# Splitting a decode over two steps: pieces of the first attention batch issued by engine, with two more raw weight tiles

## The chip, the cores and the metric

The kernel runs on one core of a Trainium2 chip. The metric is the device time of one execution in microseconds (us), as the median of several runs; shorter is better. Five engines work side by side, each through its own queue in order: PE (matrix multiplies, with PEld for its weight loads), DVE (vector work), ACT (activations), POOL and SP (here SP issues nearly all DMAs). An instruction that waits for another engine holds back everything behind it in its own queue.

## The reference, cut to what matters

Attention with rotary embedding, then a dense two-layer block, then a mixture of eight experts with one expert per row:

```python
# q, k, v: (4 batches, 8 heads, 576 rows, 64)
scores = matmul(rotate(q), rotate(k).T) / 8
attn   = softmax(scores) @ v                    # -> x (2304, 512)
h = x @ w_in; g = maximum(0.01 * h, h)          # w_in (512, 2048)
x = g @ w_out                                   # w_out (2048, 512)
e = argmax(cosine(x, expert_emb) / tau); p = softmax(...)[e]
out = p * (relu(x @ w1[e]) @ w2[e])
```

All inputs are float32, except that `w_in` and `w_out` come as pairs of 32-bit words, each tile of 128 x 512 numbers as 128 x 1024 words (512 KB): the kernel has to put the float32 number together from both words.

## The kernel before, in words

**Stages.** Attention goes through 16 pairs of heads (four pairs a batch), nine units a pair, one unit a step: 144 steps. The first four pairs (`WHOLE = 4`, the first batch, steps 0 to 35) are done in float32, the others in split float16. The dense block starts as soon as its weights and the rows of the first batch are there (from step 37 on) and then runs inside the attention steps; the experts come last.

**Side work of the first batch.** In steps 0 to 35 three kinds of side work are mixed in: the 32 raw weight tiles are decoded (`weights`, `decode`), the queries and keys of the next pair are rotated and turned (`prep_whole`), and the finished rows are scaled (`x_done`). Each is a generator that yields a `Piece` ahead of some instructions: with its cost on ACT (`A=`) and DVE (`V=`), `x=True` if it needs PE and the one PSUM buffer `t`, or `must=True` if it has to free that buffer next. A weight tile goes through: DMA; ACT L192 and L194; DVE L196 and L198; for `w_in` also ACT L220 (square sum), PE L185 (total), DVE L90 to L92 (a power of two as scale); then ACT L228 or L211 (high part) and DVE L230 or L213 (low part). Four jobs (`NW = 4`) decode at the same time, each with a raw tile of its own.

**Order.** Every step emits instructions in the order of the letters of a string. For the first batch that is `ORDER_W = 'HXtEFVCWsTsxs'`: H ACT copies the turned unit (L605), X DVE scales the scores and takes the row extreme (L575), t DVE copies the rest of the turned unit (L609), E ACT exponential (L580), F DVE finishes a unit (L645 to L649), V PE multiplies with the values (L627), C PE scores of the next two units (L551), W PE matmuls that only keep its clock up (L613), T PE turns the unit (L599). `s` is a call of `slot()`, which lets every job run one piece, and `x` one that runs PE pieces; a step also begins with `slot(must=True)`. So a job can run its ACT piece at one `s` and the DVE piece that needs it at the next `s` of the same step. `budget` caps what the decoding may issue in a step.

Of the kernel before, what the change touches and what calls it, by code (L numbers as in the profile page):

```python
# [41 lines left out]
TLOAD = 4  # L42
BUR = 1.5
WARM = 9
ORDER_W = 'HXtEFVCWsTsxs'
ORDER1 = 'HXEsFVWsLsxCs'
ORDER_A = 'ESXFHshLlVxsC'
ORDER_B = 'GXEKFHs2LVxsCo'
# [19 lines left out]
class Job:  # L68


    def __init__(self, gen):
        self.gen, self.live = gen, True
        self.run()

    def run(self):
# [21 lines left out]
def attention_moe_kernel(ctx: ExitStack, tc: tile.TileContext, qkv, w_in, w_out, emb, tau, w1, w2,  # L97
# [103 lines left out]
    slices = deque((f, o) for f in range(NF) for o in (0, 1))  # L201

    def weights(i):
        while slices:
            f, o = slices.popleft()
            raw = wp.tile([128, 512, 2], U32, name=f"raw{i}")
            if o:
                nc.sync.dma_start(out=raw.rearrange("p f t -> p (f t)"), in_=w_out32[128 * f:128 * f + 128, :])
                r = yield from decode(raw)
                yield Piece(A=0.75, when=lambda: f in M.scaled)  # L210
                nc.scalar.activation(out=wo[:, 0, f], in_=r, func=AF.Copy, scale=uw[:, f:f + 1])  # L211
                yield Piece(V=0.6)
                nc.vector.scalar_tensor_tensor(out=wo[:, 1, f], in0=r, scalar=uw[:, f:f + 1], in1=wo[:, 0, f].bitcast(F32), op0=ALU.mult, op1=ALU.subtract)  # L213
            else:
                nc.sync.dma_start(out=raw.rearrange("p (c f) t -> p c (f t)", c=4),
                                  in_=w_in32[:, 256 * f:256 * f + 256].rearrange("(c p) f -> p c f", p=128))
                w = yield from decode(raw)
                sq = small.tile([128, 1], F32, name="wsq", bufs=NW)
                yield Piece(A=0.86)
                nc.scalar.activation(out=junk[:, 0:512], in_=w, func=AF.Square, accum_out=sq, saturate=False)  # L220
                pb = yield from total(sq, 1)
                yield Piece(must=True, V=0.2)
                s = _pow2(nc, small, pb[:, 0:1], 1, uw[:, f:f + 1])
                M.scaled.add(f)
                hi = wi[:, 0, :, 128 * f:128 * f + 128]
                wv = w.rearrange("p (c f) -> p c f", c=4)
                yield Piece(A=0.75)
                nc.scalar.activation(out=hi, in_=wv, func=AF.Copy, scale=s)  # L228
                yield Piece(V=0.6)
                nc.vector.scalar_tensor_tensor(out=wi[:, 1, :, 128 * f:128 * f + 128], in0=wv, scalar=s, in1=hi, op0=ALU.mult, op1=ALU.subtract)  # L230
            M.wdone[o].add(f)
            yield Piece()
# [53 lines left out]
    def m_outs():  # L286
        while M.out:
            m_out(*M.out.pop(0))
# [379 lines left out]
    def x_done(b, c, x):  # L668

        ch = chunk[b, c]  # L670
        j = block_of[b, c]
        yield Piece(A=0.61, when=lambda: j < cur_block() + (2 * XTB if decoded() else XTB))
        sq = small.tile([128, 1], F32, name="xsq")
        nc.scalar.activation(out=junk[:, 0:512], in_=x, func=AF.Square, scale=2.0 ** 0.5, accum_out=sq, saturate=False)
        yield Piece(V=0.5)
        s = _pow2(nc, small, sq, 1, ux[:, ch:ch + 1])
        yield Piece(A=0.61)
        x16 = mp.tile([128, 2 * DM], F16, name="x16", bufs=X16)
        nc.scalar.activation(out=x16[:, 0:DM], in_=x, func=AF.Copy, scale=s)
        yield Piece(V=0.66)  # L680
        nc.vector.scalar_tensor_tensor(out=x16[:, DM:], in0=x, scalar=s, in1=x16[:, 0:DM], op0=ALU.mult, op1=ALU.subtract)
        t = blocks[j].index((b, c))
        if j not in xT:
            xT[j] = new_xt(j)
        nc.sync.dma_start_transpose(out=xT[j][:, :, 128 * t:128 * t + 128], in_=x16)
        xwait.discard(c)
        yield Piece()
        M.done.add((b, c))
        while M.ready < len(blocks) and all(z in M.done for z in blocks[M.ready]):
            M.ready += 1  # L690
# [353 lines left out]
                q.popleft()  # L1044
        return [z for z in [*list(xjobs)[:2], L.prep, *list(vjobs)[:1], *list(rjobs)[:1], *wjobs] if z is not None and z.live]

    def slot(x=False, must=False):
        used = dict(A=0.0, V=0.0)
        for z in jobs():
            p = z.nxt  # L1050
            if p.x != x or M.step < p.at or M.tick < p.tick or (p.when is not None and not p.when()):
                continue
            if x and L.x == M.tick:
                continue
            if p.must != must:
                continue
            if not p.must and z in wjobs and any(budget[e] <= 0 for e in p.cost):
                continue
            if not p.must and any(used[e] >= SLIM for e in p.cost):
                continue  # L1060
            for e, c in p.cost.items():
                budget[e] -= c
                used[e] += c
            if x:
                L.x = M.tick
            z.begun = True
            z.run()

    def step(i):

        M.tick += 1
        M.step = i if i is not None else M.step
        rate = RATE1 if M.unit == 0 else RATE2 if any(z.live for z in wjobs) else RATE3
        for e in budget:
            budget[e] = min(budget[e] + rate[e], BUR * rate[e])
        now = i is not None and 0 <= i < n
        prv = i is not None and 0 <= i - 1 < n
        due = [j for j in (i - LAGW, i - LAG) if 0 <= j < n and (j == i - LAGW) == (units[j][0] < WHOLE)] if i is not None else []
        slot(must=True)
        whole = now and units[i][0] < WHOLE  # L1080
        turned = prv and units[i - 1][0] < WHOLE
        second = M.second
        for z in ORDER_W if whole else ORDER1 if rate is RATE1 and (turned or not m_ready()) else ORDER_B if second else ORDER_A:
            if z == "E" and whole:
                a_exp(*e_[i])
            elif z == "E" and prv and not turned:
                a_exp(*e_[i - 1])
            elif z == "W":
                L.w = ps_h()
                if whole:  # L1090
                    keep_warm(0 if units[i][1] in (1, 3, 5, 8) else WARM // 2 if units[i][1] == 7 else WARM)
                elif i is not None:
                    keep_warm(WARM)
            elif z == "T" and whole:
                a_turn(i)
            elif z == "t" and turned:
                a_turned_end(*end_)
            elif z == "S":
                m = m_s1()
                M.second = bool(m or M.g or M.s)  # L1100
                if m:
                    M.h = m
            elif z == "X" and now:
                e_[i] = a_max(*units[i], ps_[i])
            elif z == "F" and L.fin and i is not None:
                a_fin(*L.fin)
                L.fin = None
            elif z == "H" and turned:
                end_ = a_turned(i - 1)
                if not whole:  # L1110
                    a_turned_end(*end_)
            elif z == "H" and prv:
                p = a_hi(e_[i - 1][0])
            elif z == "L" and prv and not turned:
                a_lo(e_.pop(i - 1)[0], p)
                pt_[i - 1] = a_transpose(p)
            elif z == "V" and due:
                g, u = units[due[0]]
                if u % 2 == 0:
                    L.o = ps_o()  # L1120
                a_pv(g, u, pt_.pop(due[0]), L.o)
                if u % 2 or u == 8:
                    L.fin = (g, u, L.o)
            elif z == "G" and M.h:
                m_g(M.h)
            elif z == "K" and M.h:
                m_leaky(M.h)
                M.g, M.h = M.h, None
            elif z == "h" and M.g:
                m_gh(M.g)  # L1130
            elif z == "l" and M.g:
                m_gl(M.g)
                M.s, M.g = M.g, None
            elif z == "C" and i is not None and 0 <= i + 1 < n:
                a_scores(i + 1)
            elif z == "2":
                M.second = False
                if M.s:
                    m_s2(M.s)
                    M.s = None  # L1140
            elif z == "o":
                m_outs()
            elif z == "x":
                slot(x=True)
            elif z == "s":
                slot()
        if R.late:
            slot()
            slot()

    wjobs += [Job(weights(i)) for i in range(NW)]
    rjobs.append(Job(directions()))
    M.step = -1
    for _ in range(PRE):
# [231 lines left out]
```

## Time and profile before

| | |
|---|---|
| median of 3 runs | 1030.99 us (1028.44 to 1032.89) |
| the profiled execution | 1032.32 us, span 1030.5 us |
| from the first X (L575) of step 0 to that of step 36 | 28.87 us to 191.88 us |
| busy in 22 to 192 us: PE / PEld / DVE / ACT | 131.99 / 107.22 / 129.55 / 122.20 of 170 us |
| granted PE clock in that stretch | 0.92 |

Read it like this: the profile page's busy shares are means over the whole span. The change touches the first batch alone, so the numbers that matter are those of its stretch. The idle time of an engine there is put down, wait by wait, to the engine that ended it.

### The profile page before, as it was taken

The numbers are of one execution on the slowest core, as the hardware profiler recorded it, in microseconds if no ns is written. First come the engines' busy times: TensorE is split into PE (matmuls) and PEld (weight loads), VectorE is DVE, ScalarE is ACT, GpSimd is POOL, SyncE is SP. The second block draws the span as 40 slices with busy tenths as digits, with TensorE's granted clock in tenths as the row PEclk, the third lists the DMA queues.
The fourth block names the chain that finished last, engine by engine and source line by source line (L and its number), as shares of the span: only waits on it lengthen the run. The fifth ranks groups of instructions, "written<-read, shape, count | busy, mean of one in ns | idle before, by whom it ended". The sixth has DMA issues, their size and how long they took to land. (4 is left out here: it accounts for less than half of the span.)

```text
span 1030.5 us, 20176 instructions
## 1 busy us (share of the span) xinstructions
PE 936.0 (91%) x7428; PEld 769.6 (75%) x7428; DVE 776.4 (75%) x1632; ACT 672.3 (65%) x1081; POOL 64.3 (6%) x64
## 2 busy tenths in 40 slices
PE   3678877899998779999899999999999999999996
PEld 2566756577886667887878888888877788888884
DVE  5786877977887867987888856422667998999992
ACT  5666777855666755766776555423256898888882
POOL 0000000000000000000000000000001462111110
PEclk9998988999998889999999999999999999999998
DMA  6333336557587667878688755200323111116190
GB/s 204 118 122 121 99 118 174 105 101 155 94 166 161 132 152 137 138 150 174 120 172 162 124 105 95 56 1 22 125 94 121 47 46 52 42 43 204 61 331 19
DMA packets 223624, 120.09 MB, mean 117 GB/s; under 512 B 194711, under 2 KB 204439, under 8 KB 223520
## 3 DMA queue, kind: packets, MB, share of 16 engines
q1 hardware_dynamic: 220320, 108.79, 45.0%
q0 software_dynamic: 3200, 9.97, 2.8%
q8 instruction: 60, 0.98, 0.4%
q14 instruction: 44, 0.36, 0.1%
HBM read 120.04 MB, written 10.49 MB: 127 GB/s over the span
## 5 line engine op out<-in xcount | busy, mean ns | idle before, releaser
L252 PEld LDWEIGHTS <-wi 128*128 128x128 f16 x1920 | 171.8, 99 | 26.9 <-issue 6.1
L282 PE MATMUL acc<-wo,gh 128*128 128x512 f32 x576 | 154.4, 411 | 2.7 <-ACT gh L266 2.6
L580 ACT ACTIVATE E<-E,amx 128x576 f32<-128x576 f32 x144 | 110.7, 769 | 34.1 <-DVE E L575 33.8
L259 ACT ACTIVATE g<-h 128x512 f32<-128x512 f32 x72 | 43.0, 598 | 136.1 <-PE h L252 57.1
L282 PEld LDWEIGHTS acc<-wo,gh 128*128 128x128 f32 x576 | 105.3, 192 | 27.1 <-ACT gh L266 4.9
L575 DVE TENSOR_SCALAR_CACHE_REDUCE E<-S,sc 128x576 f32<-128x576 f32 x108 | 87.8, 813 | 42.2 <-PE S L568 28.6
L252 PE MATMUL h<-xT,wi 128*128 128x256 f16 (+1 forms) x1152 | 113.6, 257 | 0.0
L588 DVE SCALAR_TENSOR_TENSOR P<-E,P 128x576 f16<-128x576 f32 x108 | 81.2, 752 | 16.0 <-ACT P L584 15.6
L584 ACT ACTIVATE P<-E 128x576 f16<-128x576 f32 x108 | 73.9, 684 | 29.3 <-DMA PT<-P 26.1
L252 PE MATMUL h<-xt,wi 128*128 128x256 f16 x768 | 90.7, 275 | 2.0 <-DMA xt<-x 2.0
L627 PEld LDWEIGHTS <-PT 128*128 128x128 f16 (+1 forms) x1680 | 61.4, 100 | 25.5 <-issue 14.9
L282 PE MATMUL acc<-wo,gl 128*128 128x512 f32 x288 | 77.4, 391 | 0.0
L627 PE MATMUL o<-v,PT 128*128 128x65 f16 (+3 forms) x1680 | 70.1, 194 | 7.5 <-DMA PT<-P 7.5
L566 PE MATMUL S<-stk 128*128 128x288 f16 (+1 forms) x240 | 61.2, 294 | 12.1 <-DVE E L575 10.1
L262 DVE SCALAR_TENSOR_TENSOR g<-h,g 128x512 f32<-128x512 f32 x72 | 49.5, 688 | 29.2 <-ACT g L259 29.1
L270 DVE TENSOR_TENSOR gl<-g,gh 128x512 fp32r<-128x512 f32 x72 | 49.4, 686 | 25.9 <-ACT gh L266 16.0
L282 PEld LDWEIGHTS acc<-wo,gl 128*128 128x128 f32 x288 | 54.5, 189 | 12.2
L995 PE MATMUL h<-w,hth 128*128 128x512 f32 x176 | 55.3, 395 | 0.4 <-ACT hth L979 0.4
L266 ACT ACTIVATE gh<-g 128x512 fp32r<-128x512 f32 x72 | 44.5, 618 | 15.1 <-PE acc L282 14.2
L551 PE MATMUL S<-qk 64*128 64x288 f32 (+1 forms) x96 | 30.1, 510 | 22.7 <-DVE ET L609 20.4
L568 PE MATMUL S<-stk,zq 128*128 128x288 f16 (+1 forms) x200 | 49.2, 292 | 0.0
L627 PE MATMUL o<-v,ET 128*128 128x65 f32 (+1 forms) x400 | 49.0, 275 | 0.0
(257 smaller groups left out, 1965.4 us busy)
## 6 DMA issues: line engine op xcount, KB each, us to landing
rb<-in_w SPq DMA_DIRECT2D x78, 512.0 KB
ra<-in_w SPq DMA_DIRECT2D x76, 512.0 KB
raw<-in_qkv SPq DMA_DIRECT2D x15, 640.0 KB
raw<-in_w_in SPq DMA_DIRECT2D x16, 512.0 KB
raw<-in_w_out SPq DMA_DIRECT2D x16, 512.0 KB
x2s<-x SPq DMA_DIRECT2D x18, 256.0 KB
raw<-in_qkv SPq DMA_DIRECT2D x14, 320.0 KB
v<-v SPq DMA_DIRECT2D x12, 162.5 KB
```

What stands on the lines that cost most here:

```text
L252: nc.tensor.matmul(m.h[:, c0:c1], lhsT=wi[:, a, c, 128 * f:128 * f + 128], rhs=xT[j][:, 4 * b_ + c, 0:c1 - c0], start=(n == 0), stop=(n == ...
L262: nc.vector.scalar_tensor_tensor(out=m.g, in0=m.h, scalar=0.01, in1=m.g, op0=ALU.mult, op1=ALU.max)
L270: nc.vector.tensor_tensor(out=m.gl, in0=m.g, in1=m.gh.bitcast(F32), op=ALU.subtract)
L282: nc.tensor.matmul(M.acc[:, t], lhsT=g_[:, tt], rhs=wo[:, a, f], start=(f == 0 and n == 0), stop=(f == NF - 1 and n == 2))
L566: nc.tensor.matmul(ps[o:o + m, n, 0:288], lhsT=stk[:, h, c0:c0 + m], rhs=stk[:, 2 + h, ks], start=True, stop=False)
L568: nc.tensor.matmul(ps[o:o + m, n, 0:288], lhsT=pairs[g][3][:, h, c0:c0 + m], rhs=stk[:, 4, ks], start=False, stop=True)
L575: nc.vector.tensor_scalar(out=e[:, 0:S].rearrange("p (a b) -> p a b", a=2), in0=ps[:, :, 0:288], scalar1=-0.125 if g < WHOLE else pairs[g] ...
L580: nc.scalar.activation(out=e[:, 0:S], in_=e[:, 0:S], func=AF.Exp, scale=-1.0, bias=mx)
L584: nc.scalar.activation(out=p[:, 0:576], in_=e[:, 0:S], func=AF.Copy, scale=TWO15)
L588: nc.vector.scalar_tensor_tensor(out=p[:, 576:1152], in0=e[:, 0:S], scalar=TWO15, in1=p[:, 0:576], op0=ALU.mult, op1=ALU.subtract)
L627: nc.tensor.matmul(o[ob:ob + m, 256 * h:256 * h + w], lhsT=pt[:, i, q0:q0 + m], rhs=v[:, j, h, c:c + w], start=(n == 0), stop=(n == len(to ...
L995: nc.tensor.matmul(OP[kk], lhsT=h_[:, c, :], rhs=wt[a][c // 2][:, 512 * (c % 2):512 * (c % 2) + 512], start=(n == 0), stop=(n == len(todo) ...
```

## The change

Four edits. The step order of the first batch names its calls by engine: `m` is a must call, `v` runs pieces that have DVE work or no cost, `a` pieces that have ACT work only. A job whose last piece in this step was one kind may not run one of the other kind in the same step (`z.last`); the jobs for finished rows are exempt. There are two `x` calls a step in place of one, open as long as no must piece is pending. Two further decode jobs take the two `xT` buffers as raw tiles until eight tiles are left to start, and the finished rows wait for these jobs. The higher budget (`RATE1`) ends with step 35.

```diff
-ORDER_W = 'HXtEFVCWsTsxs'
+ORDER_W = 'HXtEFxVCWmvvaTax'
+SPARE = 8
...
     def weights(i):
-        while slices:
+        while len(slices) > (SPARE if i >= NW else 0):
             f, o = slices.popleft()
-            raw = wp.tile([128, 512, 2], U32, name=f"raw{i}")
+            if i < NW:
+                raw = wp.tile([128, 512, 2], U32, name=f"raw{i}")
+            else:
+                raw = mp.tile([128, 8, 256], F16, name="xT", bufs=XTB) ...
...
-        yield Piece(A=0.61, when=lambda: j < cur_block() + (2 * XTB if decoded() else XTB))
+        yield Piece(A=0.61, when=lambda: not any(z.live for z in wjobs[NW:]) and j < cur_block() + (2 * XTB if decoded() else XTB))
...
-    def slot(x=False, must=False):
+    def slot(x=False, must=False, kind=None):
...
-            if x and L.x == M.tick:
+            if x and any(y.nxt.must for y in jobs()):
                 continue
             if p.must != must:
                 continue
+            if kind and not must:
+                if p.cost and (kind not in p.cost or (kind == "A" and "V" in p.cost)):
+                    continue
+                if z.last[0] == M.tick and z.last[1] not in (None, kind) and z not in xjobs:
+                    continue
...
-        rate = RATE1 if M.unit == 0 else RATE2 if any(z.live for z in wjobs) else RATE3
+        rate = RATE1 if M.unit == 0 and (i is None or i < 9 * WHOLE) else RATE2 if any(z.live for z in wjobs) else RATE3
...
-    wjobs += [Job(weights(i)) for i in range(NW)]
+    wjobs += [Job(weights(i)) for i in range(NW + XTB)]
```

The lines of the changed file are numbered one to four higher (L192 is L193 there, L196 L197, L211 L215, L230 L234, L575 L579, L580 L584). Both programs issue the same instructions, 144 steps each; they differ in order from the beginning up to step 41, where the last tile is done in the changed one (step 40 in the old one), and are alike from step 42 on.

**The decode of two tiles on ACT and DVE, before.** ACT in step 15: the copy H, the exponential E, the two ACT operations of tiles 817 and 819.

```order
L605 ACTIVATE ET_857<-h_843 128x512
L580 ACTIVATE E1_118<-E1_118,amx_859 128x576
L192 ACTIVATE raw0_817<-raw0_817 128x512
L194 ACTIVATE raw0_817<-raw0_817,half_88 128x512
L192 ACTIVATE raw1_819<-raw1_819 128x512
L194 ACTIVATE raw1_819<-raw1_819,half_88 128x512
```

DVE in the same step 15, from X to the X of step 16:

```order
L575 TENSOR_SCALAR E1_118,amx_859<-S_837 128x576
L609 COPY ET_857<-S_837 128x128
L645 TENSOR_SCALAR rd_863<-o_787 128x2
L648 RECIPROCAL rd_863<-rd_863 128x2
L649 TENSOR_TENSOR x1_494<-o_787,rd_863 128x128
L196 SCALAR_TENSOR_TENSOR raw0_817<-raw0_817 128x512
L198 SCALAR_TENSOR_TENSOR raw0_817<-raw0_817 128x512
L196 SCALAR_TENSOR_TENSOR raw1_819<-raw1_819 128x512
L575 TENSOR_SCALAR E0_117,amx_898<-acc_838 128x576
```

L196 of tile 817 stands in the step in which ACT's L192 and L194 of that tile stand, ahead of the X of step 16.

**The same on ACT and DVE, after.** ACT in steps 16 and 17: tiles 862 and 864 in the one, 905 and 902 in the other.

```order
L609 ACTIVATE ET_915<-h_891 128x512
L584 ACTIVATE E0_117<-E0_117,amx_917 128x576
L193 ACTIVATE raw0_862<-raw0_862 128x512
L195 ACTIVATE raw0_862<-raw0_862,half_88 128x512
L193 ACTIVATE raw2_864<-raw2_864 128x512
L195 ACTIVATE raw2_864<-raw2_864,half_88 128x512
L609 ACTIVATE ET_952<-h_931 128x512
L584 ACTIVATE E1_118<-E1_118,amx_954 128x576
L193 ACTIVATE raw1_905<-raw1_905 128x512
L195 ACTIVATE raw1_905<-raw1_905,half_88 128x512
L193 ACTIVATE raw3_902<-raw3_902 128x512
L195 ACTIVATE raw3_902<-raw3_902,half_88 128x512
```

DVE in step 18, from X to the X of step 19:

```order
L579 TENSOR_SCALAR E0_117,amx_995<-S_968 128x576
L613 COPY ET_993<-S_968 128x128
L197 SCALAR_TENSOR_TENSOR raw0_862<-raw0_862 128x512
L197 SCALAR_TENSOR_TENSOR raw1_905<-raw1_905 128x512
L199 SCALAR_TENSOR_TENSOR raw0_862<-raw0_862 128x512
L199 SCALAR_TENSOR_TENSOR raw1_905<-raw1_905 128x512
L579 TENSOR_SCALAR E1_118,amx_1042<-acc_969 128x576
```

The DVE pieces of tiles 862 and 905 moved into a step behind that of their ACT pieces: two steps later for tile 862, one for 905.

**The scale on ACT and DVE, after.** ACT in step 21, whose last instruction is the square sum of tile 907:

```order
L609 ACTIVATE ET_1132<-h_1102 128x512
L584 ACTIVATE E1_118<-E1_118,amx_1134 128x576
L215 ACTIVATE wo_101<-raw1_905,uw_82 128x512
L232 ACTIVATE wi_100<-raw3_902,ps_1128 128x4x128
L224 ACTIVATE junk_86,wsq_1115<-xT_907 128x512
```

DVE from the X of step 21 to that of step 22; the scale `pt_1166` is that of tile 907 (from PE's `t_1164`):

```order
L579 TENSOR_SCALAR E1_118,amx_1134<-acc_1062 128x576
L613 COPY ET_1132<-S_1061 128x128
L234 SCALAR_TENSOR_TENSOR wi_100<-raw0_862,ps_1082,wi_100 128x4x128
L217 SCALAR_TENSOR_TENSOR wo_101<-raw2_864,uw_82,wo_101 128x512
L91 TENSOR_SCALAR pt_1166<-t_1164 128x1
L92 TENSOR_SCALAR ps_1167<-pt_1166 128x1
L93 TENSOR_SCALAR uw_82<-pt_1166 128x1
L579 TENSOR_SCALAR E0_117,amx_1173<-S_1143 128x576
```

This part has not moved: the scale still stands ahead of the next X, and needs the last ACT work of the step before. It stands so in twelve of the 36 steps after and in thirteen before.

## Rows read from the trace of the kernel before

**Rows 1.** The page, part 2: PE's busy tenths in 40 slices, and its granted clock.
```profile
PE   3678877899998779999899999999999999999996
...
PEclk9998988999998889999999999999999999999998
```

**Rows 2.** Windows: start:end, length, busy us (count) by engine, clock, DMA share, GB/s.
```profile
22.00:192.00 170.00, 131.99 (x949) 107.22 (x950) 129.55 (x349) 122.20 (x214) 0.35 (x3) 0.92 0.39 122
...
192.00:200.00 8.00, 6.90 (x61) 5.00 (x60) 7.50 (x24) 5.83 (x12) 0.12 (x1) 1.00 0.76 133
...
208.00:216.00 8.00, 8.00 (x73) 5.97 (x72) 5.48 (x12) 5.08 (x8) 0.00 (x0) 1.00 0.88 147
```

**Rows 3.** Waits of DVE in 22 to 192: us in total, times, longest.
```profile
DVE raw L196 <- ACT raw L194: 17.4, 14, 3.1
DVE wi L230 <- ACT wi L228: 9.9, 9, 1.4
DVE pt L90 <- PE t L185: 6.2, 6, 2.2
```

**Rows 4.** Timeline of DVE: start, us, instruction [idle before]; steps 0, 15, 16, 36.
```profile
28.87 0.75 DVE L575 TENSOR_SCALAR_CACHE_REDUCE E<-S 128x576 f32<-128x576 f32 x1
...
95.91 0.75 DVE L575 TENSOR_SCALAR_CACHE_REDUCE E<-S 128x576 f32<-128x576 f32 x1
...
96.78 0.15 DVE L645 TENSOR_SCALAR rd<-o 128x2 f32<-128x2 f32 x1
...
98.79 0.69 DVE L196 SCALAR_TENSOR_TENSOR raw<-raw 128x512 uint32<-128x512 uint32 x1 [1.32 <-ACT raw L194]
...
100.12 0.69 DVE L196 SCALAR_TENSOR_TENSOR raw<-raw 128x512 uint32<-128x512 uint32 x1
100.72 0.75 DVE L575 TENSOR_SCALAR_CACHE_REDUCE E<-acc 128x576 f32<-128x576 f32 x1
...
191.88 0.81 DVE L575 TENSOR_SCALAR_CACHE_REDUCE E<-S,sc 128x576 f32<-128x576 f32 x1
```

**Rows 5.** Timeline of ACT in step 15: E, the first halves of two decodes, H.
```profile
96.76 0.78 ACT L580 ACTIVATE E<-E,amx 128x576 f32<-128x576 f32 x1 [1.01 <-DVE E L575]
97.44 0.67 ACT L192 ACTIVATE raw<-raw 128x512 f32<-128x512 f32 x1
...
98.66 0.68 ACT L192 ACTIVATE raw<-raw 128x512 f32<-128x512 f32 x1
...
99.88 0.57 ACT L605 ACTIVATE ET<-h 128x512 f32<-128x512 f32 x1
```

**Rows 6.** Timeline of DVE: start-up waits, parts of a rotation, two scale waits.
```profile
23.32 0.75 DVE L230 SCALAR_TENSOR_TENSOR wi<-raw,ps,wi 128x512 f16<-128x512 f32 x1 [0.76 <-ACT wi L228]
...
26.21 0.69 DVE L196 SCALAR_TENSOR_TENSOR raw<-raw 128x512 uint32<-128x512 uint32 x1 [1.48 <-ACT raw L194]
...
29.55 1.69 DVE L385 TENSOR_TENSOR t<-raw,tab 128x320 f32<-128x320 f32 x4
...
34.99 1.48 DVE L392 TENSOR_TENSOR raw<-raw,t 128x1280 f32<-128x1280 f32 x1
...
86.51 0.16 DVE L90 TENSOR_SCALAR pt<-t 128x1 uint32<-128x1 uint32 x1 [2.18 <-PE t L185]
...
91.95 0.16 DVE L90 TENSOR_SCALAR pt<-t 128x1 uint32<-128x1 uint32 x1 [1.40 <-PE t L185]
```

**Rows 7.** Windows of 4 us, columns as in Rows 2.
```profile
80.00:84.00 4.00, 2.15 (x21) 2.01 (x20) 3.13 (x7) 3.16 (x7) 0.00 (x0) 1.00 0.53 144
...
88.00:92.00 4.00, 4.00 (x22) 3.47 (x21) 1.82 (x5) 2.23 (x4) 0.00 (x0) 0.52 0.17 37
```

**Rows 8.** Timelines of SP and of ACT: a tile's DMA issue, and its decode.
```profile
21.00 0.38 SPq L215 DMA_DIRECT2D raw<-in_w_in  x1
...
24.87 0.66 ACT L192 ACTIVATE raw<-raw 128x512 f32<-128x512 f32 x1 [0.94 <-DMA raw<-in_w_in]
```

**Rows 9.** Waits of ACT in 22 to 192, as in Rows 3.
```profile
ACT E L580 <- DVE E L575: 32.3, 31, 1.9
```

More of the change, by code (lines that the diff above doesn't have):

```diff
@@ L71, in __init__ @@
     def __init__(self, gen):
-        self.gen, self.live = gen, True
+        self.gen, self.live, self.last = gen, True, (-9, None)
         self.run()
@@ L203, in weights @@
     def weights(i):
-        while slices:
+        while len(slices) > (SPARE if i >= NW else 0):
             f, o = slices.popleft()
-            raw = wp.tile([128, 512, 2], U32, name=f"raw{i}")
+            if i < NW:
+                raw = wp.tile([128, 512, 2], U32, name=f"raw{i}")
+            else:
+                raw = mp.tile([128, 8, 256], F16, name="xT", bufs=XTB).rearrange("p a b -> p (a b)").bitcast(U32).rearrange("p (f t) -> p f t", t=2)
             if o:
@@ L1063, in slot @@
                 used[e] += c
-            if x:
-                L.x = M.tick
             z.begun = True
+            z.last = M.tick, None if must or not p.cost else "V" if "V" in p.cost else "A"
             z.run()
@@ L1082, in step @@
         second = M.second
-        for z in ORDER_W if whole else ORDER1 if rate is RATE1 and (turned or not m_ready()) else ORDER_B if second else ORDER_A:
+        for z in ORDER_W if whole else ORDER1 if M.unit == 0 and (turned or not m_ready()) else ORDER_B if second else ORDER_A:
             if z == "E" and whole:
@@ L1142, in step @@
                 m_outs()
+            elif z == "m":
+                slot(must=True)
+            elif z in "av":
+                slot(kind=z.upper())
             elif z == "x":
```

## The prediction

> **What bounds the kernel now.** I read the page's slices first: PE is full in most of the span, but in its first fifth (eight slices of 25.8 us, up to about 206 us) it has only 3 to 8 tenths, and its clock is granted in part [rows 1]. The windows say the same for the first batch: in 22 to 192 us no engine is full, PE 132.0, DVE 129.6 and ACT 122.2 of 170 us, while from 208 us on PE has 8.00 of 8 [rows 2]. So three engines wait for each other there, and time saved in that stretch comes off the end one for one as long as PE is full behind it. The DMA queues are no bound: a share of 0.39 [rows 2], and ACT waited once for a weight tile, 0.94 us [rows 8].
>
> The list of waits says which queue loses the time. DVE waits 17.4 us for the first half of a decode (L196 for ACT's L194, 14 times), 9.9 us for the high part of a weight (L230 for L228), 6.2 us for the scale's total (L90 for PE's L185) [rows 3]. ACT in its turn waits 32.3 us for X [rows 9]; that is the other side of the same thing, since X stands in DVE's queue behind the instruction that waits. Step 15 shows it whole: ACT starts E at 96.76 and the first decode at 97.44, and is through with that at 98.66 [rows 5]; DVE has been idle since 97.47, that is 1.32 us, and its next X comes only at 100.72 [rows 4]. ACT is ready for that X after H at 99.88 and gets it late.
>
> The stretch that changes runs from the X of step 0 at 28.87 to that of step 36 at 191.88: 163.0 us, 4.53 a step [rows 4]. All waits of DVE in 22 to 192 come to 38.2 us (those of [rows 3] are 33.5; five kinds under 1.5 are the rest). Of these, 2.7 lie ahead of step 0: 0.76 and 1.48 [rows 6], and 0.5 for a scale. So DVE has 163.0 - 35.5 = 127.5 us of its own in these steps, and 35.5 of waiting.
>
> **The change, part by part.**
>
> *Pieces by engine.* The instructions are the same, and so are their durations. What goes is the wait of a DVE piece for an ACT piece of its own step: 17.4 - 1.5 (ahead of step 0) = 15.9 for L196, 9.9 - 0.8 = 9.1 for L230 [rows 3, 6]. The order shows why: L197 of tile 862 now stands two steps behind its L193, that of tile 905 one. DVE reaches such a piece after X, t and F, which in step 15 took from 95.91 to 97.47, of which X and t the time to 96.78 [rows 4]: 1.6 us into the step with an F, 0.9 without. By then ACT is normally done with the step before, for E of this step only comes after X. That is -25.0 us.
>
> *What comes in its place, ACT's surplus.* ACT and DVE now run a step apart, and where ACT has more rows than DVE for two or three steps running, DVE meets it again. I price a step by distances between starts. ACT: E 0.68, one decode 97.44 to 98.66 = 1.22, a copy H about 0.5 [rows 5]. DVE: X and t 0.87, F about 0.6, L196 or L198 0.6 [rows 4]; a rotation's first part 1.6, and its rest 2.9: the sum of 1.48 and as much for two products of the same size [rows 6]. Steps 16 to 18 after are the worst run. ACT: 0.49 + 0.68 + 2.44 = 3.6, again 3.6, and 4.6 with two copies k: 11.8. DVE: 2.5 (a rotation's first part), 4.3 (its rest and F), 3.3 (four decode instructions): 10.1. ACT is 1.7 behind at step 19, whose first L197 needs the last but two of these decodes; E hides 0.8 of it, so about 0.6 to 1.0 is waited. The same tally over all 36 steps has ACT ahead in 16 of them, by 11.8 us together. None of it is paid if each is made good in the next step, all of it if no step lends to another. I take 5, nearer to what the run of steps 16 to 18 pays (a third to a half).
>
> *The scale's round trip* is not moved: square sum on ACT at the end of a step, total on PE, L90 to L92 ahead of the next X. It is in twelve steps after and thirteen before. The six waits cost 6.2, 1.03 each, of which 5.7 are in these steps [rows 3]. A DVE that waits less elsewhere comes there sooner. Bounds: 5.7 x 12/13 = 5.3 if as many wait as now, 12 x 1.03 = 12.4 if all do. In half of the twelve steps the square sum is not ACT's last row or DVE has over 3 us of rows behind X, so I take 8, that is +2.3.
>
> *The clock in between.* Two of the six scale waits, 2.18 and 1.40 us [rows 6], lie at 86.5 and 92.0, where PE's granted clock is 0.52, nearly all at its 1.2 GHz level, after a stretch in which it had only 2.15 of 4 us [rows 7]. The mean of 0.92 [rows 2] is, with these two levels alone, some 16% of the stretch, 27 us, at the lower one. The rotation, which kept PE waiting, is now cut over two steps, so I expect fewer such dips; I leave their gain (0 to 3.6, the two waits) out of the sum and in the range. The Trainium skill (TensorE: Matmul & The Clock Gate, "HAM oscillation — how this bites in real kernels") says that a PE which keeps pausing falls back to half its clock each time; the trace agrees with it at 88 us, and by that rule shorter waits would feed on themselves, which is the fast rival below.
>
> *Two more raw tiles.* Each part of a decode now takes a step more, and six tiles in flight make up for it: the last tile is done in step 41 against step 40, and from step 42 on both orders are alike. The price is DMA: a tile's load issued at 21.00 was waited for until 24.87, 3.9 us [rows 8]. A decode stands at least two steps, now some 8 us, behind its load, so it is covered, and I take 0; the other end is the slower rival below. The two extra loads at the start replace that wait of 0.94, and one more tile's L196 and L198 (1.2 us) come ahead of step 0: X of step 0 stays within a microsecond of 28.87. One tile less is left in the stretch for it, so this cancels.
>
> *PE's second x call and the place of T* change no count: k follows its turn as before. *The lower budget from step 36 on* leaves the dense block's first unit in the same step 37; DVE has 7.50 of 8 us there [rows 2] and the same rows to do in steps 36 to 41 (some 17 us before, 16 after), so nothing is gained or lost there.
>
> Sum: -25.0 + 5 + 2.3 = -17.7, and with a little for the dips about -19: the stretch takes 144 us in place of 163, 4.0 a step. Against the profiled execution's 1032.32 that is 1013.3; it stands 1.3 above the median of the runs, so **1012 us**.
>
> **The rivals.**
>
> *Carried over whole.* ACT's surplus is paid in full (11.8) and every scale waits (12.4 - 5.7 = 6.7): -25.0 + 18.5 = -6.5, 1024.5. For it: three engines at 72 to 78% leave little slack for a shift between them [rows 2]. Against: wherever a piece's ACT work is already done DVE does not wait, as at L196 of 100.12 and the X behind it [rows 4], and full payment needs every surplus to fall on a step that cannot lend.
>
> *DVE alone.* Waits for L194 and L228 go, and so do the scale's, as PE's clock stays up: -25.0 - 5.7 = -30.7, near 1000 to 1001. For it: the dips follow PE's pauses. Against: PE itself has 132.0 busy us [rows 2], more than DVE's 127.5.
>
> *It does not do what it says.* DVE gets to each piece earlier by as much as the piece was moved, and waits there again: 1031. Against: X gates both E and the pieces, so ACT's last step is closed before DVE's pieces of the next come up.
>
> *Slower: the tiles come in bursts.* After, six loads are issued within three to five steps twice, and four within two or three steps twice. If a tile landed at the stretch's mean rate of 122 GB/s [rows 2], it would take 4.3 us, the last of six 25.8, while it is due 16 us after the first (two loads a step of 4 us, two steps of grace): 9.8 late; the last of four, 17.2 against 12, 5.2. Two of each: 30 us, and ACT's L193, which waits, holds E behind it. -19 + 30 = +11, 1042. It decides above 24 us of lateness, which means tiles of about 4 us, that is under 135 GB/s. Against: four tiles in flight have cost 0.94 us so far [rows 8], and 122 is a mean over idle time too: by the share of 0.39 busy engines move 313 GB/s, 1.7 us a tile [rows 2].
>
> **How the numbers follow.** Forecast 60% (its own range 1004 to 1020), carried over 15%, DVE alone 13%, no effect 7%, slower 5%. The range goes from DVE alone to carried over: 1001 to 1025. A measurement of this kernel tells about 0.5%, 5 us, from no change: faster than 1025.8 are the forecast, DVE alone and most of carried over, 85%; within it the rest and no effect, 10%; slower 5%.
>
> **What would show it.** In the changed profile X of step 0 stays near 29 us and that of step 36 comes near 172. In that stretch L197 waits for L195 under 4 us in all and L234 for L232 under 2; L91 for PE's total 6 to 10; ACT's wait for X falls from 32 to under 20; PE's granted clock rises to 0.94 or more. From step 42 on every row comes earlier by the same amount. If L197 still waits over 10 us, the step apart is not enough; if L193 waits for the DMA over 5 us, the tiles are late; if the stretch is shorter and the end is not, the time is given back behind step 36, where I saw nothing that could.

## The result, and the profile after

The changed kernel takes **1018.47 us** (median of 4 runs, 1016.56 to 1020.86) against 1031.94 of the kernel before beside it (4 runs): 0.9875 of its time, with an interval of 0.9841 to 0.991. It is 13.5 us faster. The forecast was 1012, range 1001 to 1025. Its profiled execution took 1019.13 us, with a span of 1017.3 (before: 1030.5).

I take the rows in the order of the prediction. First the X of step 0 and of step 36 on DVE (timeline: start, us, instruction, idle before it); they answer to the first and last of [rows 4].

```profile
29.01 0.75 DVE L579 TENSOR_SCALAR_CACHE_REDUCE E<-S 128x576 f32<-128x576 f32 x1
...
178.53 0.81 DVE L579 TENSOR_SCALAR_CACHE_REDUCE E<-S,sc 128x576 f32<-128x576 f32 x1
```

The stretch between them takes 149.5 us in place of 163.0: 13.5 less, all of the gain. Behind it nothing is lost or won: X comes 12.8 us earlier at step 41 (197.67 against 210.45), 13.1 at step 143, and the span ends 13.2 earlier. The same stretch in one window (length, then busy us by engine, clock, DMA share, GB/s; compare [rows 2]):

```profile
29.00:178.50 149.50, 126.82 (x932) 104.88 (x933) 123.15 (x339) 116.67 (x210) 0.35 (x3) 0.92 0.39 118
```

The granted clock is 0.92 as before, not 0.94 or more. Now all that DVE waits for in that window (us in total, times, longest), against [rows 3]:

```profile
DVE pt L91 <- PE t L186: 10.0, 11, 2.1
DVE ET L613 <- PE S L603: 8.2, 5, 3.2
DVE E L579 <- PE S L603: 5.6, 6, 1.3
```

Both waits for ACT that stood at the top of [rows 3] are gone in full: no instruction of DVE waits for L195 or L232. But the scale's total is waited for 10.0 us, and a wait that was small before (L609 and L575 for PE's S, 1.9 us in this stretch) has grown to 13.8: DVE waits for T, PE's transposes of E. ACT's own waits in the stretch:

```profile
ACT E L584 <- DVE E L579: 14.0, 17, 2.4
ACT qk L414 <- PE t L407: 6.2, 3, 2.7
ACT ET L609 <- PE h L603: 6.0, 7, 1.7
...
ACT raw L193 <- DMA raw<-in_w_in: 1.3, 1, 1.3
```

ACT's wait for X has fallen from 32.3 [rows 9] to 14.0. A weight tile was late once, by 1.3 us: the two raw tiles cost nothing.

Where the new wait lies is seen in step 10, which takes 7.95 us (67.14 to 75.09; before, 3.98). DVE:

```profile
67.14 0.75 DVE L579 TENSOR_SCALAR_CACHE_REDUCE E<-acc 128x576 f32<-128x576 f32 x1
...
71.08 0.29 DVE L613 COPY ET<-S 128x128 f32<-128x128 f32 x1 [3.18 <-PE S L603]
...
75.09 0.76 DVE L579 TENSOR_SCALAR_CACHE_REDUCE E<-S 128x576 f32<-128x576 f32 x1 [1.31 <-PE S L603]
```

and PE (L407 is a turn of the rotation, L631 is V, L617 the clock matmuls W, L603 is T):

```profile
63.82 0.66 PE L407 MATMUL t<-idn,raw 128*128 128x128 f32 x4 [1.55 <-DVE raw L396]
65.16 0.87 PE L407 MATMUL t<-idn,raw 128*128 128x128 f32 x4 [0.69 <-ACT qk L414]
65.83 2.24 PE L631 MATMUL o<-v,ET 128*128 128x65 f32 x10
67.86 2.12 PE L617 MATMUL h<-ones 128*128 128x256 f16 x9
69.78 1.06 PE L603 MATMUL h<-idn,E 128*128 128x128 f32 x4
70.63 0.42 PE L603 MATMUL S<-idn,E 128*128 128x128 f32 x1
...
74.89 1.23 PE L631 MATMUL o<-v,ET 128*128 128x65 f32 x10
75.95 1.15 PE L617 MATMUL h<-ones 128*128 128x256 f16 x9
```

Two things stand in this list. The turns wait, 1.55 us at the end of step 9 and 0.69 in the early x call of step 10, and V, W and T, which DVE's next rows need, are queued behind them on PE: the second four turns are the second x call of a step, put ahead of V. And what follows runs at half speed: ten V take 2.24 us where the same ten take 1.23 at 74.89, nine W 2.12 against 1.15. The windows give the clock (columns as above):

```profile
60.00:64.00 4.00, 2.12 (x15) 1.49 (x16) 3.90 (x8) 2.02 (x3) 0.00 (x0) 1.00 0.55 188
64.00:68.00 4.00, 3.31 (x19) 3.08 (x19) 3.90 (x9) 3.44 (x6) 0.00 (x0) 0.68 0.41 124
68.00:72.00 4.00, 4.00 (x22) 3.14 (x21) 0.85 (x5) 0.49 (x2) 0.00 (x0) 0.50 0.43 138
```

PE had 2.12 of 4 us, then its clock fell to 0.50, the lower of its two levels (1.2 GHz), and DVE and ACT, with 0.85 and 0.49 of 4 us, nearly stood still. Step 19 (6.98 us) is the same, at a granted clock of 0.70 in 104 to 108.

### The profile page after: what moved, and what is told of

It reads as the page before. It is cut to its first block, busy times and chain, and to the rows that moved or that the text cites. A ratio compares the mean times of both kernels' runs of the same rounds, so it can differ in the third digit from the quotient of the medians.

```text
span 1017.3 us, 20125 instructions
## 1 busy us (share of the span) xinstructions
PE 936.5 (92%) x7428; PEld 770.1 (76%) x7428; DVE 775.1 (76%) x1632; ACT 670.0 (66%) x1081; POOL 63.4 (6%) x64
## 5 line engine op out<-in xcount | busy, mean ns | idle before, releaser
L579 DVE TENSOR_SCALAR_CACHE_REDUCE E<-S,sc 128x576 f32<-128x576 f32 x108 | 87.8, 813 | 44.3 <-PE S L572 29.3
L584 ACT ACTIVATE E<-E,amx 128x576 f32<-128x576 f32 x144 | 110.7, 769 | 15.7 <-DVE E L579 15.6
L631 PEld LDWEIGHTS <-PT 128*128 128x128 f16 (+1 forms) x1680 | 61.4, 100 | 25.1 <-issue 14.9
L631 PE MATMUL o<-v,PT 128*128 128x65 f16 (+3 forms) x1680 | 70.1, 194 | 6.9 <-DMA PT<-P 6.8
L570 PE MATMUL S<-stk 128*128 128x288 f16 (+1 forms) x240 | 61.5, 295 | 10.3 <-DVE E L579 10.0
L286 PEld LDWEIGHTS acc<-wo,gl 128*128 128x128 f32 x288 | 54.6, 190 | 12.2
L631 PE MATMUL o<-v,ET 128*128 128x65 f32 (+1 forms) x400 | 49.7, 276 | 0.0
L933 DVE TENSOR_TENSOR w<-rb,w 128x1024 fp32r<-128x1024 f32 x40 | 46.3, 1220 | 3.4 <-ACT w L932 2.6
```

Of the source, the lines that this page charges most:

```text
L286: nc.tensor.matmul(M.acc[:, t], lhsT=g_[:, tt], rhs=wo[:, a, f], start=(f == 0 and n == 0), stop=(f == NF - 1 and n == 2))
L570: nc.tensor.matmul(ps[o:o + m, n, 0:288], lhsT=stk[:, h, c0:c0 + m], rhs=stk[:, 2 + h, ks], start=True, stop=False)
L579: nc.vector.tensor_scalar(out=e[:, 0:S].rearrange("p (a b) -> p a b", a=2), in0=ps[:, :, 0:288], scalar1=-0.125 if g < WHOLE else pairs[g] ...
L584: nc.scalar.activation(out=e[:, 0:S], in_=e[:, 0:S], func=AF.Exp, scale=-1.0, bias=mx)
L631: nc.tensor.matmul(o[ob:ob + m, 256 * h:256 * h + w], lhsT=pt[:, i, q0:q0 + m], rhs=v[:, j, h, c:c + w], start=(n == 0), stop=(n == len(to ...
```

## The experiments

Two theories for the missing 5 us of the stretch. **Queue** (Q): the early x call puts turns, which wait, ahead of V, W and T in PE's order. **Clock**: the order is harmless, and what costs is that PE falls to 1.2 GHz after its waits for the rotation. Beside them stood whether the change's two halves (the order by engine, the six tiles) each carry part of the gain, and what the scale's round trip costs. Ratios are to the kernel before, run on the same chip; "stretch" is X of step 0 to X of step 36 in the profiled execution.

| | us | ratio, interval | stretch | DVE waits in it: scale; T |
|---|---|---|---|---|
| after | 1018.47 | 0.9875, 0.9841 to 0.991 | 149.5 | 10.0; 13.8 |
| one x a step | 1007.84 | 0.9761, 0.9724 to 0.9799 | 142.1 | 10.4; 9.1 |
| four tiles | 1027.57 | 0.9959, 0.9941 to 0.9977 | 139.1 | 10.1; 13.7 |
| old order, six tiles | 1043.7 | 1.0104, 1.007 to 1.0138 | 180.6 | 2.9; 1.5 |
| warm turn | 1017.0 | 0.9852, 0.9816 to 0.9887 | 146.1 | 10.3; 10.2 |
| one x + warm turn | 1007.79 | 0.977, 0.9754 to 0.9786 | 141.0 | 10.5; 6.8 |
| late must | 1006.61 | 0.9752, 0.9729 to 0.9774 | 137.3 | 2.6; 12.9 |
| all three | 1004.7 | 0.9753, 0.9729 to 0.9778 | 133.9 | 2.9; 9.2 |
| warm in every step | 1017.86 | 0.987, 0.9846 to 0.9894 | 147.8 | 11.6; 10.5 |
| all three + that | 1000.59 | 0.9694, 0.9668 to 0.972 | 139.3 | 2.9; 14.6 |

Each stretch, and each wait in it, is read from one profiled execution. Two of the very same kernel (all three, which was run twice) gave 133.9 and 136.1 us, with 9.2 and 11.6 us of waiting for T: differences of some 2 us in these two columns tell nothing.

**One x a step.** The changed kernel without its early x call, and with the old rule of one such piece a step:

```diff
-ORDER_W = 'HXtEFxVCWmvvaTax'
+ORDER_W = 'HXtEFVCWmvvaTax'
-            if x and any(y.nxt.must for y in jobs()):
+            if x and L.x == M.tick:
...
+            if x:
+                L.x = M.tick
```

> The changed kernel, with the PE pieces of a step as they were: one x call at the step's end, one PE piece a step. Theory Q (queue order): DVE's new waits for T (13.8 us of L613 and L579 for L603 in the changed kernel) come from the second turn of a rotation, which the early x puts ahead of V, W and T in PE's queue; without it these waits fall below 4 us and the stretch from X of step 0 to X of step 36 is 140 to 144 us in place of 149.5, the time some 6 us under the changed kernel's 1018. Theory C (clock): they come from PE's fall to 1.2 GHz after it has waited for the rotation, whatever the order; they stay over 9 us and the time is within 4 us of the changed kernel's. The last tile is then done in step 43 in place of 41.

The stretch is 7.4 us shorter and the total 1.1% lower, with intervals apart: the early call costs. Of the 7.4, 4.7 is waiting for T (13.8 to 9.1) and 3.4 is DVE's own time, of which some 2.5 are four decode instructions that fall behind step 36 (some 24 tiles in the stretch, not 25); other waits grew by 0.7. The moved instructions were not paid for later: by step 41 this kernel is 9.8 ahead. But the wait for T is not under the 4 us that queue forecast, and the stretch's clock is 0.94 in place of 0.92, so how much of the gain is the queue's alone is not shown. Step 19 falls from 6.98 to 4.02. But step 10 still takes 6.85, with the clock at 0.50 in 68 to 72, so clock is not refuted.

**Four tiles.** The changed kernel without the two extra jobs:

```diff
-    wjobs += [Job(weights(i)) for i in range(NW + XTB)]
+    wjobs += [Job(weights(i)) for i in range(NW)]
```

> The changed kernel without the two further decode jobs: four raw tiles as before, pieces ordered by engine. If the order by engine alone makes the gain, the first 36 steps are as short as in the changed kernel or shorter (149.5 us or less). If the two tiles are needed with it, what is gained is given back behind: the order shows the last tile done in step 61 in place of 41, and the dense block's units that come later by it lengthen the rest. I expect 142 to 150 us for the stretch and a total between 1022 and 1040, that is the first theory for the stretch and the second for the whole.

Within 0.5% of the kernel before. Its stretch is the shorter for holding some 20 tiles in place of some 25; the last is done in step 61, and from X of step 36 to the end it takes 859.4 us, after 838.8. A piece a step later without tiles to cover it only moves decode out behind step 36, where PE is full.

**Old order, six tiles.** The other half alone: the order and x rule of the kernel before, with the rest of the change.

```diff
-ORDER_W = 'HXtEFxVCWmvvaTax'
+ORDER_W = 'HXtEFVCWsTsxs'
```

> The two further raw tiles alone: six decode jobs in the old step order, with the old rule of one PE piece a step. If the tiles make the gain by themselves, 1018. If the order by engine does, DVE still waits for ACT's L195 and L232 (over 18 us of the 25) and the time is 1024 to 1034; the last tile is done in step 33, which by itself takes DVE rows out of steps 36 to 40 and puts them ahead.

It is 1.0% slower (its profiled execution, 1050.53 us, is the longest of its six runs). The waits for ACT in its stretch are those of before, and more of them:

```profile
DVE raw L197 <- ACT raw L195: 26.2, 17, 3.5
DVE wi L234 <- ACT wi L232: 8.3, 9, 1.3
```

So the order takes the waits away, and the tiles alone take away none. The granted clock in this stretch is 0.78, against 0.92 in the kernel before, so how much of the 1.0% the tiles cost and how much the clock is not shown. Neither half is worth much by itself (-0.4% and +1.0%); together they give -1.25%.

**Warm turn.** The changed kernel, with nine clock matmuls ahead of a rotation's first turn, so that PE has work before what it waited for:

```diff
+                if t == 0:
+                    for _ in range(WARM):
+                        nc.tensor.matmul(pt[:, 0:256], lhsT=ones16[:, 0:128], rhs=ones16, start=True, stop=True)
```

> The changed kernel with nine further clock matmuls (the same as in W) ahead of a rotation's first turn, into the turn's own PSUM tile, where PE waits for DVE's L396 anyway. Theory C: PE's granted clock no longer falls at steps 10 and 19 (0.50 and 0.70 in the changed kernel's windows 68:72 and 104:108), DVE's waits for T there (3.2 and 2.4 us) fall under 1 us each, and the stretch is 143 to 146 us in place of 149.5, the total 1012 to 1015. Theory Q: the nine matmuls cost a microsecond or so of PE at each of three turns and nothing is won: 1018 to 1021.

Where it was put it did what clock said: step 10 takes 4.70 us in place of 7.95 with the same instructions otherwise, and step 19 5.32 in place of 6.98. DVE's timeline of that step, beside that of the changed kernel above:

```profile
67.72 0.75 DVE L582 TENSOR_SCALAR_CACHE_REDUCE E<-acc 128x576 f32<-128x576 f32 x1
...
69.02 0.29 DVE L616 COPY ET<-S 128x128 f32<-128x128 f32 x1 [0.55 <-PE S L606]
...
72.42 0.76 DVE L582 TENSOR_SCALAR_CACHE_REDUCE E<-S 128x576 f32<-128x576 f32 x1 [0.71 <-PE S L606]
```

and the windows, as above:

```profile
64.00:68.00 4.00, 2.92 (x25) 2.62 (x26) 4.00 (x9) 2.92 (x6) 0.00 (x0) 1.00 0.28 66
68.00:72.00 4.00, 4.00 (x44) 3.26 (x42) 3.09 (x9) 3.30 (x6) 0.12 (x1) 1.00 0.99 303
```

The clock stays at 1.00 there and the two waits for T shrink from 4.49 to 1.26 us. Over the stretch the gain is 3.4; its mean clock is no higher (0.90), as the clock falls elsewhere (0.57 in 156 to 160), and in the total the gain can't be told from nothing, where 1012 to 1015 had been expected.

**One x and warm turn** together (the edits of both):

> One PE piece a step at its end (as in the kernel that took 1007.8) and, with it, the nine further clock matmuls ahead of a rotation's first turn. If place in PE's queue and clock are two causes, their gains add: some 3 us under 1007.8, the stretch 138 to 140 us against 142.3, and PE's granted clock no longer at 0.50 in 68 to 72. If the one x call has taken away what the clock matmuls gained, 1006 to 1009 and the stretch as it was.

Step 10 is down from 6.85 to 4.01, with the order on DVE and ACT unchanged. So in this one step the clock is worth about 3 us in either order (7.95 to 4.70, 6.85 to 4.01). The total is that of one x alone; in the stretch the two edits give 8.5 us together, 7.4 and 3.4 alone, which is too near to the spread of the profiles to say whether they add.

**Late must.** The scale's total is used by a call at the head of each step, ahead of X; here, in steps of the first batch, only the call `m` in the order does it, behind X, V and W:

```diff
-        slot(must=True)
         whole = now and units[i][0] < WHOLE
+        if not whole:
+            slot(must=True)
```

> The changed kernel without the must call at the head of a step of the first batch; the one at m, behind X, E and C, stays. The scale (L91 to L93) then stands behind X, t and F on DVE, the copy k behind H and E on ACT, and the early x finds a must pending, so that turns go to the step's end. Theory R (round trip): DVE's 10.0 us of waiting for the scale's total go nearly all (under 3 left), ACT's wait for turns (6.2 and 5.4 us of L414 and L417) falls under 4 together, and the stretch is 130 to 136 us against 149.5, the total 999 to 1004: the gain of the kernel with one x call and some 8 us on top. If PE's clock is what decides, the waits move to L613 and L579 for T and the total is 1006 to 1010.

The scale's wait goes from 10.0 to 2.6 (L91 0.7, and 1.9 that X waits, by the trace, for the same total), the stretch from 149.5 to 137.3, the total down by 1.2%. As in one x, four decode instructions fall behind step 36 and are not paid for there: from X of step 36 to the end are 839.0 us, after 838.8.

Not all of this is the scale's. As its expectation says, the early x call now finds a must piece pending, and the turns go to the step's end: in the trace PE's instructions stand in the very order of one x, from the first to the last. So late must is one x with the scale moved as well, and has to be compared with it. Against one x the total can't be told apart (0.9752 and 0.9761), and the stretch is 4.8 us shorter: the scale's wait falls from 10.4 to 2.6 while that for T rises from 9.1 to 12.9. In step 34, where PE runs at 0.50 to 0.53 in both, one x waits 3.51 us for the scale and late must 3.37 for T: one delay of PE, met at another instruction.

**All three** (one x, late must, warm turn):

> One x call, the must call behind X, and the clock matmuls ahead of the first turn, all three. If the three causes add up, 996 to 1001, the stretch 126 to 132 us, near DVE's own rows (123 us busy). If PE's clock is no longer lost once the queues do not wait for each other, the clock matmuls add nothing to the kernel with the late must call.

The total can't be told from late must alone. The two hold the same instructions in the same order on PE, DVE and ACT, but for the 27 clock matmuls ahead of three turns. That leaves the clock as what differs in step 34. There both kernels run the same rows, and PE comes to W in both after a wait of the same length for ACT. PE's timeline, late must:

```profile
150.78 2.08 PE L617 MATMUL h<-ones 128*128 128x256 f16 x9 [1.64 <-ACT ET L609]
...
153.71 2.24 PE L631 MATMUL o<-v,ET 128*128 128x65 f32 x10
155.88 2.19 PE L555 MATMUL S<-qk 64*64 64x288 f32 x8
```

and DVE's, the X of step 34 and of step 35:

```profile
152.06 0.75 DVE L579 TENSOR_SCALAR_CACHE_REDUCE E<-acc 128x576 f32<-128x576 f32 x1
...
160.14 0.76 DVE L579 TENSOR_SCALAR_CACHE_REDUCE E<-S 128x576 f32<-128x576 f32 x1 [3.37 <-PE S L603]
```

All three, PE and then DVE in the same way:

```profile
151.40 1.14 PE L620 MATMUL h<-ones 128*128 128x256 f16 x9 [1.65 <-ACT ET L612]
...
152.92 1.23 PE L634 MATMUL o<-v,ET 128*128 128x65 f32 x10
154.08 1.19 PE L558 MATMUL S<-qk 64*64 64x288 f32 x8
```

DVE:

```profile
152.67 0.75 DVE L582 TENSOR_SCALAR_CACHE_REDUCE E<-acc 128x576 f32<-128x576 f32 x1
...
156.40 0.76 DVE L582 TENSOR_SCALAR_CACHE_REDUCE E<-S 128x576 f32<-128x576 f32 x1 [0.25 <-PE S L606]
```

The step takes 8.08 us at the lower level and 3.73 at the higher: this dip costs 4.35 us in a step whose DVE work is about 3.5. The last 4 us ahead of W, late must:

```profile
146.78:150.78 4.00, 1.83 (x16) 1.72 (x17) 2.68 (x9) 4.00 (x8) 0.00 (x0) 0.89 0.97 282
```

All three:

```profile
147.40:151.40 4.00, 1.99 (x18) 1.71 (x16) 2.66 (x9) 4.00 (x8) 0.00 (x0) 1.00 0.69 202
```

PE was busy for 1.83 and 1.99 us, and only the first clock fell. In the second profile of all three (the run on another chip, below) it fell too, behind a pause of the same 1.65 us; PE, and the X of steps 34 and 35:

```profile
149.75 2.08 PE L620 MATMUL h<-ones 128*128 128x256 f16 x9 [1.65 <-ACT ET L612]
```

```profile
151.02 0.75 DVE L582 TENSOR_SCALAR_CACHE_REDUCE E<-acc 128x576 f32<-128x576 f32 x1
...
159.01 0.76 DVE L582 TENSOR_SCALAR_CACHE_REDUCE E<-S 128x576 f32<-128x576 f32 x1 [3.28 <-PE S L606]
```

So one and the same program takes 3.73 us for this step in one execution and 8.0 in another: a dip comes and goes without any edit. The Trainium skill (TensorE: Matmul & The Clock Gate, "HAM oscillation — how this bites in real kernels") describes a kernel in which each DMA wait of some 3 to 5 us between its matmuls drops PE to half its clock. Here shorter pauses do it: one of some 1.65 us did in two of these three profiles and not in the third, so the length of the pause alone does not tell where a dip comes; what does is not shown.

**Warm in every step.** Four clock matmuls in the steps that had none (units 1, 3, 5 and 8 of a pair), on the changed kernel and on all three:

```diff
-                    keep_warm(0 if units[i][1] in (1, 3, 5, 8) else WARM // 2 if units[i][1] == 7 else WARM)
+                    keep_warm(WARM // 2 if units[i][1] in (1, 3, 5, 8) else WARM // 2 if units[i][1] == 7 else WARM)
```

> The changed kernel with four clock matmuls in those steps of the first batch that had none (units 1, 3, 5 and 8 of a pair), 16 steps, some 0.45 us of PE each at the high clock. Theory C: PE's granted clock stays up (the mean of the stretch 0.96 or more against 0.92), DVE's waits for T (13.8 us in the changed kernel) fall to 4 to 8 us, the total is 1009 to 1014 in place of 1018. Theory Q: PE's queue is what delays T, so four matmuls more ahead of it add up to 7 us: 1019 to 1025.

> The same four clock matmuls in the kernel with one x call, late must call and clock matmuls ahead of the turn (1004.7). If the rest of DVE's waits for T (9.2 us there) comes from the clock: 998 to 1002. If PE has no room left in a step of 3.7 us: 1005 to 1010.

On the changed kernel the stretch's clock rises from 0.92 to 0.97, the stretch falls only from 149.5 to 147.8 (in the fastest of its five runs), and the time stays: 0.987. So the mean clock by itself is not what the 5 us hang on: DVE waits for T 10.5 us even so. On all three it looked like 0.6% (0.9694), measured on another chip, so both were run once more side by side:

> The kernel with one x call, late must call and clock matmuls ahead of the turn once more, on the same chip and beside the same runs of the kernel before as its sister with four clock matmuls in the odd steps: was the distance of 4 us between them (1004.7 and 1000.6, from two chips) the clock matmuls' or the chips'? If the clock matmuls': 1003 to 1006 here, and the first-batch stretch is longer than the sister's. If not: both within 2 us of each other.

> The sister with four clock matmuls in the odd steps too. If they gain: 999 to 1002 and a first-batch stretch under that of the kernel without them, with a higher granted clock. If, as in its first profile (stretch 139.3 against 133.9 us, clock 0.93 against 0.95), they do not: within 2 us of it or above.

All three gave 1002.48 us, 0.973 (0.9704 to 0.9755), with the matmuls 1001.1, 0.9712 (0.9686 to 0.9738). The distance of 1.4 us is inside both intervals: no gain shown. In the stretch the matmuls cost: 139.3 against 133.9 in the first pair, 139.1 against 136.1 in the second. From X of step 36 to the end, where both programs issue the same, they are 6.4 us quicker in both pairs (830.8 against 837.2, 831.1 against 837.5), most of it between steps 68 and 80; why is not shown. Either version beats both kernels of this case, the one before by 2.7 to 2.9%, the changed one, by the ratios, by some 1.5%.

## Why the prediction was right, and where it was not

The measured time lies in the range, and the largest term was right. That it came so near to the forecast is in part luck: waits that the prediction did not see were offset by a cost that was not paid and by small gains that it had not counted.

*Pieces by engine, -25.0.* Right in full. DVE waits for neither ACT half in the stretch; old order shows that it is the order that does it.

*ACT's surplus, +5.* Wrong: 0.0 us. The run of steps 16 to 18, from which I took it, shows no wait for L195 either. I set ACT's rows against DVE's alone, but DVE loses 24 us to PE in these steps, and in that time ACT can catch up (that this is how it came is my reading; no run tests it alone, and in all three, where DVE's waits are down to 12.2 us, it still does not wait for L195).

*The scale's round trip, +2.3.* The mechanism was right, the size was not: 5.6 became 10.0, that is +4.4, inside the bounds of 5.3 and 12.4. Eleven of the scales now wait. What it is worth in the total is not shown: late must takes nearly all of this wait away, but the total is that of one x, whose order of PE it shares.

*The clock in between, 0 to -3.6.* This is the step that failed. I wrote that a rotation cut over two steps would make fewer dips, left their gain out of the sum and yet put 1.3 of it in (-17.7 became -19); the clock stayed at 0.92, and DVE's wait for T, which I had no term for, rose from 1.9 to 13.8: +11.9. Two causes are shown: the place of the turns ahead of V, W and T (one x: 4.7 less of it, and 1.1% of the total) and the halved speed behind a pause (warm turn: 3.6 less, and 3 us of step 10 with the order unchanged). I had looked at "PE's second x call" for its count alone, "no change", and not for what it stands ahead of in a queue that runs in order. How the whole splits between clock and plain dependence stays open, because the dips move with each edit, and even between two executions of one program.

*Raw tiles and DMA, 0.* Right: 1.3 us late once, against the 24 us at which the slower rival would have decided (its tiles of 4 us are 131 GB/s, not 135). *X of step 0 near 29*: 29.01. I expected one tile more ahead of it to make it later and the stretch shorter by as much; X came no later, and the stretch holds just one of the two-word decode instructions less (49 against 50, some 0.6 us). DVE's own time in it is 2.0 us shorter; the rest lies in shorter distances between the same instructions (the last section has one kind).

The account of the stretch: -25.0 + 4.4 (scale) + 11.9 (T) - 2.8 (three small waits of before, for the stg, v and square sum of ACT) - 2.0 (own time) = -13.5. The forecast's -19 lay 5.5 off, since 15.3 of waits came that I had not in the sum (13.2 for T, with the 1.3 I had set against it for the dips, and 2.1 more of the scale), while a surplus of 5 was not paid and 4.8 of small gains (2.8 and 2.0) had not been counted. *Carried over whole* (1024.5) let nearly as much waiting come back as did (18.5 against 16.3 us), but most of it as ACT's surplus, which did not come.

*Behind step 36*: nothing lost, as forecast (13.35 earlier at step 36, 12.8 at step 41, 13.2 at the end). *DVE alone* (1000 to 1001) is nearly what the last kernels reach, 1001 to 1005, once turns, scale and clock were dealt with. That does not bear out its mechanism: in all three DVE still waits 12.2 us in the stretch, and the time comes near that price with 6 us less of DVE's own work there.

## What to carry to other kernels

When three engines at three quarters wait for each other, a wait that is taken away from one of them comes back in part at the next dependence in line (16.3 of 25.0 us here): price the gain less the waits on the third engine, and read the order of that engine's queue for what a waiting piece is put ahead of. A call moved earlier is not neutral because its count is the same. A deeper pipeline needs the buffers and the order together: either half alone gave next to nothing here, or a loss. Before an edit is credited with a gain, see from the order of every queue what else it moved: late must moved PE's turns too.

## What the runs showed of the hardware that was not expected

One dip of PE's clock, in a step of 3.73 us, cost 4.35 us, more than the step: V, the clock matmuls and T stand in one chain on PE, and all of them take nearly twice as long (nine clock matmuls 1.14 to 2.08 us, ten V 1.23 to 2.24, eight score matmuls 1.19 to 2.19). The clock matmuls that are there to prevent a dip take 0.94 us longer themselves once it has come. A dip elsewhere cost nothing: in the second profile of all three steps 0 and 1 ran at 0.50 and 0.54 and took 2.3 and 4.6 us, in late must at 1.00 2.3 and 4.7.

Two dependent DVE instructions on one tile start 0.72 us apart (L196 at 98.79, L198 at 99.51 in the kernel before; 0.72 to 0.73 in all twelve such pairs of its stretch with no wait between), the same pair on two tiles in turn 0.60 (below, changed kernel, step 10): 0.12 us for each pair that is interleaved. Before:

```profile
99.51 0.69 DVE L198 SCALAR_TENSOR_TENSOR raw<-raw 128x512 uint32<-128x512 uint32 x1
```

After:

```profile
71.89 0.68 DVE L197 SCALAR_TENSOR_TENSOR raw<-raw 128x512 uint32<-128x512 uint32 x1
72.48 0.69 DVE L199 SCALAR_TENSOR_TENSOR xT<-xT 128x512 uint32<-128x512 uint32 x1
73.09 0.69 DVE L199 SCALAR_TENSOR_TENSOR raw<-raw 128x512 uint32<-128x512 uint32 x1
```
